# Order of the feed forward's units, and the layout of the weights' maxima on their way through DRAM

## The chip, the cores and the metric

The kernel runs on one core of one Trainium2 chip. The metric is the device time of one execution in microseconds (us); the median of three runs of the kernel before is 1657.21 us (1657.04 to 1657.3). Five engines work at once, each through its own instructions in order: TensorE (PE, matrix products; its weight loads are listed as PEld), VectorE (DVE), ScalarE (ACT), GpSimd (POOL) and SyncE (SP), which here issues every transfer. They meet through semaphores.

## The reference

One transformer block with conditioning, over 2048 rows of 512 values. Three steps are cut to what matters:

```
mod = silu(c) @ w_mod, cut into sa, ca, ga, sb, cb, gb
h = layernorm(x) * (1 + ca) + sa
q = h @ wq                                   # 32 heads of 128
p = softmax(q k^T / sqrt(128))               # over the last 512 rows of the cache, per head
x = x + ga * (concat(p v) @ wo)
h = layernorm(x) * (1 + cb) + sb
x = x + gb * ((gelu(h @ w_gate) * (h @ w_up)) @ w_down)      # 1376 hidden columns
```

## The kernel before, in words

**Precision.** Every operand of a product is held as two 16-bit halves, a high one and a low one, and a product is three matmuls: high by high, high by low, low by high. Before it is split, a weight matrix is scaled by a factor that depends on its largest absolute value. That maximum has to be known on all 128 partitions; bringing it there is called a crossing.

**Attention.** The 32 heads are taken in 16 groups of two, and the 2048 rows in four row groups of 512 (0 to 3). `slot` (L1294) runs the 128 pairs of a head and a row group as a pipeline: scores, row maxima (DVE), exponentials (ACT), the low half of the probabilities (POOL, tile `pp`), a transpose by transfer (SP, tile `pT`), the product with v two slots later, the product with wo three slots later, and the sum into `acc` (DVE). While one group of heads runs, the weights of the next are loaded into `raw`, their maxima are taken (`h_max` L649, into `mx`), crossed, and the weights scaled (`h_scale` L750) and split.

**The crossings.** From the third group of heads on, a crossing goes through DRAM. `h_send` (L663) writes four columns of maxima, one per matrix, of 128 partitions to a DRAM tile `most` of 128 rows of four values. `spread_max` (L667) reads the 512 values back to every partition (tile `sa`, 256 KB), reduces each kind's 128 values to one (tile `top`, four values on each partition), and makes the scale and its inverse from them (`iv` and `av`). There are two for each of 14 groups of heads (wq with k, v with wo) and one for the feed forward's weights (`ff_cross` L1255, `ff_scalars` L1269), 29 in all.

**Feed forward.** The 1376 hidden columns are 11 blocks f of 128 (the last of 96). Row groups 0 and 1 form pair 0, 2 and 3 pair 1. Blocks 0 and 1 of pair 0 are computed plainly (`fill`). All else is done in units (p, f): one block f for both row groups of a pair p, by seven products of halves in place of eight (Strassen's scheme in Winograd's form; `product` L1558, `stage` L1678). A unit is 7 x 6 = 42 matmuls. It needs the weights of its block as seven pieces with high and low halves, tile `aw`, of which three exist at a time (L1479, in the ring `pT`). `aw_load` brings gate and up weights in, and `aw_make` (L1822) scales two tiles, makes four sums on POOL, six high halves on ACT and six low halves on POOL. The left-hand pieces of a pair (tiles named B.. and T..) come from the second layer norm of its row groups; for pair 1 these steps are entered with units (0,2), (0,3) and (0,4) (`P1`, L1843).

The results of a unit become hidden tiles (`hid`, a ring of eight places, L1341). When both blocks of f and f + 1 of a pair are done, eight down steps (f, f + 1) by w_down are queued, one for each 128 rows, each of 6 matmuls and one sum into `acc` on DVE. After each of the four stages of a unit, one down step is taken from the queue (`down`, L1720). Blocks 0 to 3 of pair 1 are put through another scheme, in seven steps for two blocks.

The loop over `UNITS` (L1851) says for each unit which weights are made in it: `SPLIT` lists the units that have weights of their own, and a unit with index k in `SPLIT` makes those of index k + 2 and loads those of k + 4, unless `MAKE` says otherwise. A unit of pair 1 that isn't in `SPLIT` uses the weights of the same block of pair 0 (`AW[u if u in AW else (0, f)]`).

**What sets the order.** The program doesn't issue instructions as it goes. A planner (class `Weaver`) collects all of them with their dependencies and an estimated length each (`cost` L150), plays the whole program through on a model of the engines in several stages (`CUTS` L95) with a fixed number of turns and of random shakes from a fixed seed, and then issues the best order that it found (`issue` L412). Operations given with two engines (`either`, `tt`) get one of the two in that play. So the profile shows one line, L444, for nearly all instructions, and one reads it by the names of tiles. The rings of tiles and of PSUM banks tie the order of units: a unit's products use `psS`, of which two exist. Whatever changes in the program changes the input of the planner, and the order anywhere may change with it.

Of the kernel before, what the change touches and what calls it, by code (L numbers as in the profile page):

```python
# [10 lines left out]
F32 = mybir.dt.float32  # L11
# [3 lines left out]
OP = mybir.AluOpType  # L15
AX = mybir.AxisListType
PSUM = bass.MemoryType.PSUM

P = 128
# [10 lines left out]
NF = (DFF + P - 1) // P  # L30
# [15 lines left out]
ROUND = 1.0 + 2.0 ** -7  # L46
# [405 lines left out]
def adaln_block(ctx: ExitStack, tc: tile.TileContext, x, k_cache, v_cache, wq, wo,  # L452
                w_gate, w_up, w_down, c_in, w_mod, out):
    nc = Weaver(tc.nc, tc)
# [7 lines left out]
    dram = nc.pool(ctx.enter_context(tc.tile_pool(name="dram", bufs=1, space=bass.MemoryType.DRAM)), True, True)  # L462
# [7 lines left out]
    def small(pool, cols_, bufs=3, name="sm"):  # L470
        return pool.tile([P, cols_], F32, name=name, tag=name, bufs=bufs)
# [172 lines left out]
    HW, DG, IV, AV, ES, RV = {}, {}, {}, {}, {}, {}  # L644
# [16 lines left out]
            IV[kh], AV[kh] = iv[:, i:i + 1], av[:, i:i + 1]  # L661

    def h_send(which, m):  # L663
        t = DG[which[0]] = dram.tile([P, 4], F32, name="most", tag="most", bufs=3)
        nc.sync.dma_start(t, m[:, 0:4])

    def spread_max(t, top):  # L667
        w = right.tile([P, N], F32, name="sa", tag="sa", bufs=1)
        nc.sync.dma_start(w, t.rearrange("p a -> (p a)").partition_broadcast(P))
        r = small(base, 4, 2, "top")  # L670
        nc.vector.tensor_reduce(r, w.rearrange("p (k a) -> p a k", a=4), op=OP.max, axis=AX.X)
        iv, av = small(base, 8, 5, "iv"), small(base, 8, 5, "av")
        nc.vector.tensor_scalar(iv[:, 0:4], r, 1e-30, ROUND / top, op0=OP.max, op1=OP.mult)
        nc.vector.reciprocal(av[:, 0:4], iv[:, 0:4])
        return iv, av

    def h_spread(which):
        iv, av = spread_max(DG.pop(which[0]), WQS if which[0][0] in SETS[0] else WS)
        for i, kh in enumerate(which):
            IV[kh], AV[kh] = iv[:, i:i + 1], av[:, i:i + 1]  # L680
# [354 lines left out]
    def at(half, f, *a):  # L1035
        bg.setdefault(half, []).append((f, a))
# [43 lines left out]
    for g in range(1, NG):  # L1080
        b = 2 * PER * (g - 1)
        steps, cross_at = (STEPS, CROSS) if g > 1 else (EARLY, (EARLY_CROSS, (11, 13)))
        for i, kinds in enumerate(SETS):
            which = [(kind, g * G + n) for kind in kinds for n in range(G)]
            for m, (kind, h) in enumerate(which):
                st = steps[kind, h % G]
                at(b + st[0], load_raw, kind, h)
                if kind == "wo" and g >= GATED:
                    at(b + st[1], h_gate, h)
                at(b + st[1], h_max, (kind, h), mxs[i], m)  # L1090
                if (kind, h % G) == (kinds[-1], G - 1):
                    at(b + cross_at[i][0] + (g > 1) * 1.125, *((h_send, which, mxs[i]) if g > 1 else (h_cross_a, which, mxs[i])))
                    at(b + cross_at[i][1] + (g > 1) * 1.125, h_spread if g > 1 else h_cross_b, which)
                    for n in range(G):
                        at(b + cross_at[i][1] + (g > 1) * 1.25, h_scalars, g * G + n, ("qk", "vo")[i])
            for kind, h in which:
                st = steps[kind, h % G]
                at(b + st[2], h_scale, kind, h)
                if kind != "wq" or g < WINO:
                    at(b + st[3], h_split, kind, h)  # L1100
                if kind == "k":
                    at(b + st[4], h_turn, h)
        if g >= WINO:
            for half, f, nm in ((4, a_sum, "S1"), (5, a_split, "A1"), (5, a_sum, "S2"), (6, a_split, "S1"), (6, a_sum, "S3"),
                                (7, a_split, "S2"), (7, a_sum, "S4"), (8, a_split, "S3"), (8, a_split, "A22"),
                                (9, a_split, "S4")):
                at(b + half, f, g, nm)
# [147 lines left out]
    def ff_cross():  # L1255
        m = mxf
        for i in range(2):
            nc.vector.tensor_reduce(m[:, i:i + 1], mff[:, 12 * i:12 * i + 12], op=OP.max, axis=AX.X)
        nc.vector.tensor_reduce(m[:, 2:3], mff[:, 24:40], op=OP.max, axis=AX.X)
        for i in range(2):  # L1260
            nc.vector.tensor_reduce(m[:, 3 + i:4 + i], cols[:, 8 + 4 * i:12 + 4 * i], op=OP.max, axis=AX.X,
                                    apply_absolute_value=True)
        nc.vector.tensor_tensor(m[:, 3:4], m[:, 3:4], m[:, 4:5], op=OP.add)
        h_send(("f", "f", "f", "f"), m)
# [4 lines left out]
    def ff_scalars(part):  # L1269
        ab, t = ffs[:, 6:7], ffs[:, 7:8]  # L1270
        if part == 0:
            FS["iv"], av = spread_max(DG.pop("f"), WS)
            nc.vector.tensor_scalar_mul(ffs[:, 0:2], av[:, 0:2], 0.5)
            nc.vector.tensor_scalar_mul(ffs[:, 2:3], av[:, 2:3], 0.5)
            nc.vector.tensor_scalar(ab, FS["iv"][:, 3:4], WS, 1e-25, op0=OP.mult, op1=OP.max)
        iv = FS["iv"]
        if part == 1:
            nc.vector.tensor_scalar(ffs[:, 3:4], ab, iv[:, 0:1], 2.0 / HS, op0=OP.mult, op1=OP.mult)
            nc.vector.tensor_scalar(t, ab, iv[:, 0:1], 2.0, op0=OP.mult, op1=OP.mult)
            nc.vector.tensor_scalar(ffs[:, 5:6], ab, iv[:, 1:2], 4.0 * HID / HS, op0=OP.mult, op1=OP.mult)  # L1280
            nc.vector.tensor_scalar(ffs[:, 5:6], ffs[:, 5:6], iv[:, 2:3], t, op0=OP.mult, op1=OP.mult)
        if part == 2:
            nc.vector.tensor_scalar_mul(t, t, HID)
            nc.vector.reciprocal(ffs[:, 4:5], t)
            nc.vector.reciprocal(ffs[:, 8:9], ab)
            nc.vector.tensor_scalar(cols[:, 8:16], cols[:, 8:16], ffs[:, 8:9], HS, op0=OP.mult, op1=OP.mult)
# [53 lines left out]
    PLAIN = 2  # L1340
# [160 lines left out]
    def aw_load(u):  # L1501
        ff_load(u[1], u)
# [257 lines left out]
    for c, (a, b, d) in enumerate(((15.5, 15, 16.25), (15, 16.25, 16.5), (16.5, 16, 17.25), (16, 17.25, 17.5))):  # L1760
        at(e + a, ln2_chunk, 0, c)
        at(e + b, ln2_high, 0, c)
        at(e + d, ln2_low, 0, c, nc.gpsimd)
    UNITS = [(0, f) for f in range(PLAIN, 8)] + [(1, 6), (1, 7)] + [(p, f) for f in range(8, NF - 1) for p in range(2)] + \
        [(0, NF - 1)] + [(1, f) for f in range(6)] + [(1, NF - 1)]
    MAKE = {(0, 7): None, (1, 7): 7, (0, 8): 8, (0, 9): 9, (0, 10): 10}
    SPLIT = [u for u in UNITS if not (u[0] and 6 <= u[1] < NF - 1)]
    at(e + 10, aw_load, UNITS[0])
    at(e + 11, aw_load, UNITS[1])
    at(e + 16, aw_scale, UNITS[0])  # L1770
    for n in range(4):
        at(e + 17, aw_sum, UNITS[0], n)
    for n, nm in enumerate(AWS):
        h = (18.5, 18, 19.5, 19, 20.5, 20, 21.5, 21)
        at(e + h[n], aw_high, UNITS[0], nm)
        at(e + h[n + 1], aw_low, UNITS[0], nm)
# [45 lines left out]
    def aw_make(u):  # L1822
        aw_scale(u)
        for n in range(4):
            aw_sum(u, n)
        for nm in AWS:
            aw_high(u, nm)
            aw_low(u, nm)
# [22 lines left out]
    for n, u in enumerate(UNITS):  # L1851
        p, f = u
        k = SPLIT.index(u) if u in SPLIT else None
        k = MAKE.get(u, None if k is None else k + 2)
        if k is not None:
            if k + 2 < len(SPLIT):
                aw_load(SPLIT[k + 2])
            if k < len(SPLIT):
                aw_make(SPLIT[k])
        if WDS:  # L1860
            w = WDS.pop(0)
# [63 lines left out]
```

## Time and profile before

| | |
|---|---|
| median of three runs | 1657.21 us |
| the profiled execution, its own time | 1657.58 us |
| its span | 1655.8 us |
| mean granted TensorE clock | 0.997 |
| waits of TensorE from 1340 us on | 0.6 us on POOL (B), 0.5 us on ACT (r), 0.4 us on DVE (r) |
| waits of TensorE from 200 to 1300 us | 0.2 us on the transfer pT |
| sends of maxima (`most`) / spreads (`sa`) | 29 / 29 |
| median from issue to landing, send / spread | 1.9 us (28 of them) / 3.8 us |
| DVE's waits for a spread | 7.2 us, 8 times |

The span is the profiled execution from its first to its last instruction. "A <- B" in a wait says that A waited for B. In groups of instructions, "x29 | 31.6, 1089" is the count, the busy time in us and the mean length in ns, and what follows is idle time of the engine ahead of them and what ended it. Lines in order of time begin with the start and the length in us, and a bracket gives the idle time ahead. A matmul is listed with 379 ns because it overlaps with its neighbours; what one takes of TensorE's time is read from the count in a stretch without idle.

### The profile page before, as it was taken

What the parts mean: (1) busy time and instruction counts of PE and PEld (TensorE: products, weight loads), DVE (VectorE), ACT (ScalarE), POOL (GpSimd) and SP (SyncE); (2) the same over time, 40 slices, a digit from 0 to 9 for tenths busy, and PEclk for the clock granted to TensorE, in tenths of its full rate; (3) what the DMA queues carried; (4) which work ended last, traced back from release to release, by engine and by line L of the source; (5) the groups of instructions that cost most, each with busy time, mean ns of one, the idle gap of its engine ahead of it and who ended that gap; (6) DMA issues with size and microseconds to landing.
All of it is one profiled execution on the core that took longest, in us unless ns stands there. A gap on an engine that the chain in (4) does not pass through costs nothing.

```text
span 1655.8 us, 24293 instructions
## 1 busy us (share of the span) xinstructions
PE 1642.4 (99%) x7732; PEld 764.5 (46%) x7732; DVE 1289.3 (78%) x2381; ACT 1216.6 (73%) x2418; POOL 1305.0 (79%) x1097
## 2 busy tenths in 40 slices
PE   8999999999999999999999999999999999999999
PEld 4444444444444444444444444444444444444455
DVE  7777787878787788788999887888887956656557
ACT  5987797777787777888778777787878876545451
POOL 5999986868586878787768889999977898784682
PEclk9999999999999999999999999999999999999999
DMA  7676697878787778999999997788877712101111
GB/s 241 128 144 130 135 157 143 152 138 149 144 143 140 153 136 157 186 196 194 196 200 205 189 167 148 147 175 179 168 129 158 144 28 64 42 25 51 42 45 52
DMA packets 686289, 228.61 MB, mean 138 GB/s; under 512 B 596432, under 2 KB 663056, under 8 KB 686160
## 3 DMA queue, kind: packets, MB, share of 16 engines
q1 hardware_dynamic: 686160, 227.05, 69.1%
q8 instruction: 61, 1.00, 0.3%
q14 instruction: 68, 0.56, 0.1%
HBM read 78.98 MB, written 5.38 MB: 51 GB/s over the span
## 4 chain that ended last, share of the span: by engine, by line
PE 91%; ACT 2%; POOL 2%; DVE 2%; DMA 1%; SPq 1%; issue 1%; DVEq 0%; POOLq 0%; ACTq 0%
PE psS L444 31%; PE psW L444 23%; PE psO L444 21%; PE psQ L444 17%; SPq L444 1%; DVE st L444 1%; DVE acc L444 1%; DMA pT<-pp 1%; ACT p L444 0%; POOL pp L444 0%; POOL B L444 0%; DMA wm<-in_w_mod_dram 0%; POOL aw L444 0%; ACT T L444 0%; DMA raw<-in_B_w_up_dram 0%
## 5 line engine op out<-in xcount | busy, mean ns | idle before, releaser
L444 POOL TENSOR_TENSOR pp<-p,pp 128x1024 f16<-128x1024 f32 x256 | 545.9, 2132 | 212.8 <-ACT pp L444 97.3
L444 ACT ACTIVATE p<-psS,st,es 128x512 f32<-128x512 f32 x512 | 393.4, 774 | 187.7 <-DVE st L444 186.8
L444 DVE SCALAR_TENSOR_TENSOR acc<-psW,st,acc 128x512 f32<-128x512 f32 x496 | 367.2, 742 | 79.8 <-PE psW L444 77.7
L444 PE MATMUL psW<-wo,oT 128*128 128x512 f16 x1536 | 416.3, 379 | 0.0
L444 PE MATMUL psS<-kT,q 128*128 128x512 f16 x1536 | 379.1, 379 | 2.0 <-ACT q L444 2.0
L444 PE MATMUL psO<-pT,v 128*128 128x512 f16 x1536 | 377.1, 379 | 0.3 <-DMA pT<-pp 0.2
L444 DVE TENSOR_REDUCE st<-psS 128x2 f32<-128x1024 f32 x256 | 312.5, 1221 | 60.0 <-PE psS L444 59.6
L444 ACT ACTIVATE pp<-p 128x1024 f16<-128x1024 f32 x256 | 271.0, 1059 | 3.7
L444 PEld LDWEIGHTS <-q 128*128 128x128 f16 x1536 | 149.9, 98 | 182.1 <-ACT q L444 2.6
L444 PEld LDWEIGHTS <-v 128*128 128x128 f16 x1536 | 150.0, 98 | 181.3 <-DMA pT<-pp 1.2
L444 PEld LDWEIGHTS <-oT 128*128 128x128 f16 x1536 | 150.2, 98 | 180.1 <-DVE oT L444 0.5
L444 PEld LDWEIGHTS <-aw 128*128 128x128 f16 (+1 forms) x840 | 84.2, 100 | 95.1 <-issue 2.0
L444 ACT ACTIVATE oT<-psO 128x512 f16<-128x512 f32 x128 | 76.1, 594 | 66.2 <-PE psO L444 66.1
L444 PE MATMUL psQ<-T,S 128*128 128x512 f16 x504 | 123.3, 379 | 0.0
L444 PE MATMUL psQ<-B,A 128*128 128x512 f16 x480 | 119.6, 381 | 0.1
L444 PE MATMUL psS<-T,aw 128*128 128x512 f16 (+1 forms) x480 | 116.9, 379 | 0.0
L444 DVE SCALAR_TENSOR_TENSOR oT<-psO,oT 128x512 f16<-128x512 f32 x128 | 88.0, 688 | 30.9 <-ACT oT L444 30.6
L444 PEld LDWEIGHTS <-A 128*128 128x128 f16 x696 | 68.3, 98 | 83.3 <-issue 2.3
L444 PEld LDWEIGHTS <-S 128*128 128x128 f16 x672 | 65.8, 98 | 79.3
L444 ACT ACTIVATION_READ_ACCUMULATOR p<-psS,st,es 128x1 f32 x512 | 101.0, 197 | 0.0
L444 POOL TENSOR_TENSOR q<-h,q 128x512 f16<-128x512 f32 x84 | 97.5, 1161 | 2.0 <-ACT q L444 1.8
L444 DVE TENSOR_REDUCE mx<-raw 128x1 f32<-128x512 f32 x128 | 84.2, 674 | 15.6 <-DMA raw<-in_A_wq_dram 9.1
(211 smaller groups left out, 2295.6 us busy)
## 6 DMA issues: line engine op xcount, KB each, us to landing
raw<-in_A_k_cache_dram SPq DMA_DIRECT2D x32, 256.0 KB, 3.9
raw<-in_A_wq_dram SPq DMA_DIRECT2D x32, 256.0 KB, 3.7
raw<-in_A_v_cache_dram SPq DMA_DIRECT2D x32, 256.0 KB, 3.3
raw<-in_A_wo_dram SPq DMA_DIRECT2D x32, 256.0 KB, 3.2
pT<-pp SPq DMA_TRANSPOSE x512, 3.3
sa<-most SPq DMA_DIRECT2D x29, 256.0 KB, 3.8
raw<-in_B_w_gate_dram SPq DMA_DIRECT2D x24, 256.0 KB, 3.1
raw<-in_B_w_up_dram SPq DMA_DIRECT2D x24, 256.0 KB, 3.4
```

The costliest lines, as they stand in the source:

```text
L444: made[n] = real(*a, **k)
```

## The change: what it does

Two edits in one.

The units of the feed forward come in another order. Before: (0,2) to (0,7), (1,6), (1,7), (0,8), (1,8), (0,9), (1,9), (0,10), (1,0) to (1,5), (1,10). After: (0,2) to (0,9), (1,8), (1,9), (0,10), (1,6), (1,7), (1,0) to (1,5), (1,10). The units of pair 1 that use the weights of pair 0 are then (1,8) and (1,9), in place of (1,6) to (1,9); (1,6) and (1,7) are loaded and made once more. `SPLIT` has 18 entries in place of 16, and `MAKE` is written anew: no weights are made in (0,9) and in (1,8), those of (1,6) in (1,9), and from there on one set in each unit as long as there are any.

The DRAM tile of a crossing is laid out by kind: four rows of 128 values in place of 128 rows of four. The send writes each value by itself to its place, the read back is the same 512 values in a row, and the reduction takes 128 neighbours for each kind where it took every fourth value. The scale `iv` is computed by POOL, not by DVE; its inverse `av` stays on DVE.

```diff
     def h_send(which, m):
-        t = DG[which[0]] = dram.tile([P, 4], F32, name="most", tag="most", bufs=3)
-        nc.sync.dma_start(t, m[:, 0:4])
+        t = DG[which[0]] = dram.tile([4, P], F32, name="most", tag="most", bufs=3)
+        nc.sync.dma_start(t.rearrange("a p -> p a"), m[:, 0:4])
 
     def spread_max(t, top):
         w = right.tile([P, N], F32, name="sa", tag="sa", bufs=1)
-        nc.sync.dma_start(w, t.rearrange("p a -> (p a)").partition_broadcast(P))
+        nc.sync.dma_start(w, t.rearrange("a p -> (a p)").partition_broadcast(P))
         r = small(base, 4, 2, "top")
-        nc.vector.tensor_reduce(r, w.rearrange("p (k a) -> p a k", a=4), op=OP.max, axis=AX.X)
+        nc.vector.tensor_reduce(r, w.rearrange("p (a k) -> p a k", a=4), op=OP.max, axis=AX.X)
         iv, av = small(base, 8, 5, "iv"), small(base, 8, 5, "av")
-        nc.vector.tensor_scalar(iv[:, 0:4], r, 1e-30, ROUND / top, op0=OP.max, op1=OP.mult)
+        nc.gpsimd.tensor_scalar(iv[:, 0:4], r, 1e-30, ROUND / top, op0=OP.max, op1=OP.mult)
         nc.vector.reciprocal(av[:, 0:4], iv[:, 0:4])
...
-    UNITS = [(0, f) for f in range(PLAIN, 8)] + [(1, 6), (1, 7)] + [(p, f) for f in range(8, NF - 1) for p in range(2)] + \
-        [(0, NF - 1)] + [(1, f) for f in range(6)] + [(1, NF - 1)]
-    MAKE = {(0, 7): None, (1, 7): 7, (0, 8): 8, (0, 9): 9, (0, 10): 10}
-    SPLIT = [u for u in UNITS if not (u[0] and 6 <= u[1] < NF - 1)]
+    UNITS = [(0, f) for f in range(PLAIN, NF - 1)] + [(1, NF - 3), (1, NF - 2), (0, NF - 1), (1, 6), (1, 7)] + \
+        [(1, f) for f in range(6)] + [(1, NF - 1)]
+    MAKE = {(0, 9): None, (1, 9): 9}
+    SPLIT = [u for u in UNITS if not (u[0] and NF - 3 <= u[1] < NF - 1)]
```

## The prediction

> **What bounds the kernel now.** I read the page's totals first, then the busy time in stretches of 40 us, then TensorE's own waits in the feed forward, then the groups of instructions there, and last the transfers of the crossings.
>
> ```profile
> span 1655.8 us, 24293 instructions
> PE 1642.4 (99%) x7732; PEld 764.5 (46%) x7732; DVE 1289.3 (78%) x2381; ACT 1216.6 (73%) x2418; POOL 1305.0 (79%) x1097
> ...
> PE 91%; ACT 2%; POOL 2%; DVE 2%; DMA 1%; SPq 1%; issue 1%; DVEq 0%; POOLq 0%; ACTq 0%
> ```
>
> TensorE works for 1642.4 of 1655.8 us, and 91% of the chain that ended last is its own work. It idles 13.4 us in all. Where, the stretches tell (columns: stretch, its length, then the busy time and count of each engine, granted clock, DMA share, GB/s):
>
> ```profile
> 0.00:40.00 40.00, 33.54 (x156) 20.08 (x156) 29.06 (x76) 20.76 (x35) 20.25 (x40) 0.91 0.80 250
> 40.00:80.00 40.00, 38.88 (x195) 19.66 (x196) 32.77 (x66) 39.87 (x80) 37.53 (x31) 1.00 0.69 128
> ...
> 600.00:640.00 40.00, 40.00 (x187) 18.11 (x185) 31.79 (x60) 29.73 (x62) 31.49 (x25) 1.00 0.75 144
> ...
> 1320.00:1360.00 40.00, 39.40 (x199) 19.77 (x197) 27.16 (x47) 31.15 (x54) 36.29 (x40) 1.00 0.22 54
> ...
> 1440.00:1480.00 40.00, 39.03 (x180) 17.39 (x178) 25.40 (x33) 21.03 (x40) 32.13 (x31) 1.00 0.10 27
> ...
> 1640.00:1680.00 40.00, 11.84 (x55) 5.17 (x53) 8.94 (x14) 0.63 (x1) 0.00 (x0) 0.95 0.14 53
> ```
>
> The start loses 6.46 + 1.12 = 7.58 us, before any instruction that the change touches. The last matmul ends at 1651.84, and 1655.8 - 1651.84 = 3.96 us of last sums and stores follow. The stretch from 600 stands for the attention: no idle, 187 matmuls in 40 us, so 0.214 us each. The feed forward loses 0.60 us near 1345 and 0.97 us after 1440, 1.57 us together. What is left, 13.4 - 7.58 - 3.96 - 1.57 = 0.3 us, is spread over 1240 us of attention. The change neither adds nor takes a matmul, so **its whole reach is the waits: about 1.6 us at best, 0.1% of the time**, unless it makes new ones.
>
> TensorE's longest wait from 1340 on, then the two waits after 1440 in order of time with the POOL work beside them:
>
> ```profile
> PE psS L444 <- POOL B L444: 0.6, 1, 0.6
> ```
>
> ```profile
> 1353.88 0.59 PE L444 MATMUL psS<-B,aw 128*128 128x512 f16 x2
> ...
> 1462.95 1.46 PE L444 MATMUL psS<-B,aw 128*128 128x512 f16 x6 [0.39 <-DVE r L444]
> ...
> 1463.61 1.16 POOL L444 TENSOR_TENSOR T<-ft,T 128x512 f16<-128x512 f32 x1
> ...
> 1467.51 0.81 PE L444 MATMUL psS<-B,aw 128*128 128x512 f16 x3 [0.52 <-ACT r L444]
> ```
>
> The waits of 0.39 and 0.52 us stand in units (1,6) and (1,7), the first two of the second pair. POOL is still writing that pair's T tiles at 1464.77, while their products run; the down steps that could fill the gap had been spent. The wait of 0.60 us is on a tile of the plain blocks, ahead of the first unit, which starts at 1353.88.
>
> **The order of units.** The change puts (0,8) and (0,9) ahead of the second pair's first unit, which becomes (1,8). A unit is 42 matmuls, 42 x 0.214 = 9.0 us, and four down steps of 6 matmuls, 5.1 us. So the T tiles are due 2 x 14.1 = 28 us later, and both waits lose their cause: **-0.91 us**; with the 0.05 us beside them -0.97, which I take. Not below zero gain by this edit, not above 1.57.
>
> Pair 1's units (1,6) and (1,7) no longer share weights with (0,6) and (0,7), so two sets more are loaded, scaled, summed and split. Rows of the feed forward's groups:
>
> ```profile
> L444 POOL TENSOR_TENSOR aw<-raw,aw 128x512 f16<-128x512 f32 x14 | 17.2, 1232 | 23.3 <-ACT aw L444 14.9 <-DVE r L444 7.5 <-ACT r L444 0.9
> L444 ACT ACTIVATE raw<-raw,ffs 128x512 f32<-128x512 f32 x23 | 16.1, 709 | 0.4 <-DMA raw<-in_B_w_up_dram 0.4
> L444 POOL TENSOR_TENSOR S1f<-raw 128x256 f32<-128x256 f32 x13 | 11.2, 860 | 3.3 <-issue 1.3 <-ACT r L444 1.2 <-POOL aw L444 0.7
> L444 POOL TENSOR_TENSOR aw<-S4f,aw 128x256 f16<-128x256 f32 x14 | 10.3, 737 | 2.4 <-DVE r L444 1.8 <-DVE hf L444 0.6
> L444 ACT ACTIVATE aw<-raw 128x512 f16<-128x512 f32 x14 | 8.7, 623 | 11.1 <-PE psS L444 11.0
> L444 ACT ACTIVATE aw<-S3f 128x256 f16<-128x256 f32 x14 | 5.7, 409 | 1.1 <-POOL S3f L444 0.9
> ```
>
> POOL, each set: four sums at no more than 0.860, one low half at 1.232, five at no more than 0.737: 8.4 us. ACT: two scalings at 0.709, one high half at 0.623, five at 0.409: 4.1 us. Two sets: 16.8 us of POOL, 8.2 of ACT. They fall in (1,9) and (0,10), since the ring of three weight tiles frees a place only when (1,8) and then (1,9) are through: nine units of 14.1 us after 1353.9, from about 1481 on. What stood there before, and what the busiest stretch stood:
>
> ```profile
> 1354.00:1431.00 77.00, 77.00 (x372) 36.70 (x370) 47.72 (x67) 51.10 (x95) 65.15 (x77) 1.00 0.17 47
> 1431.00:1470.00 39.00, 38.03 (x175) 16.99 (x174) 24.59 (x33) 18.89 (x34) 32.60 (x30) 1.00 0.10 28
> 1470.00:1500.00 30.00, 30.00 (x141) 13.60 (x139) 17.30 (x24) 15.88 (x31) 20.76 (x28) 1.00 0.19 51
> 1500.00:1530.00 30.00, 30.00 (x141) 14.04 (x139) 19.82 (x27) 17.81 (x35) 12.58 (x17) 1.00 0.16 44
> 1530.00:1570.00 40.00, 40.00 (x187) 18.74 (x186) 20.50 (x29) 18.44 (x37) 25.35 (x33) 1.00 0.13 37
> ```
>
> POOL (the fifth count and the time ahead of it) is free for 17.4 + 14.7 = 32 us from 1500 to 1570 and a part of the 9.2 us ahead of them; 16.8 us fit. From 1354 to 1431, POOL at 65.15 of 77 us (85%) with a set made in nearly every unit cost TensorE nothing. So I take **0**; without that cover it is what the 84% of 1431:1470 cost, 0.97 us. The four loads join DMA engines that are at most 0.19 busy there; the four issues on SP stand two units ahead of their use. 0.
>
> The down queue no longer stands empty in one unit, as it did in (0,9), so four steps fewer are left behind the last unit. The last product and the first matmul on the last unit's hidden tile:
>
> ```profile
> 1631.89 1.46 PE L444 MATMUL psS<-T,aw 128*96 128x512 f16 x6
> ...
> 1640.89 0.68 DVE L444 TENSOR_TENSOR hid<-r,hid 96x512 f16<-96x512 f32 x1
> ...
> 1645.85 0.81 PE L444 MATMUL psO<-wd,hid 96*128 96x512 f16 x3
> ```
>
> The cover is 1645.85 - 1633.35 = 12.5 us; less 4 x 6 x 0.214 = 5.1 it is 7.4. The first hidden tile was ready at 1641.57, 8.2 us after the product, with additions of the down steps in between on DVE; four of those go too. I take **0**; by the order as it stands it would cost 0.8 us.
>
> **The crossings.** All 29 are off TensorE's path unless a queue holds. Sending the maxima becomes 512 single values in place of 128 runs of four; the reduction reads neighbours; one line of four values moves from DVE to POOL.
>
> ```profile
> L444 DVE TENSOR_REDUCE mx<-raw 128x1 f32<-128x512 f32 x128 | 84.2, 674 | 15.6 <-DMA raw<-in_A_wq_dram 9.1 <-DMA raw<-in_A_k_cache_dram 4.8 <-POOL raw L444 1.1
> L444 DVE TENSOR_REDUCE top<-sa 128x4 f32<-128x512 f32 x29 | 31.6, 1089 | 7.3 <-DMA sa<-most 7.2
> L444 DVE TENSOR_SCALAR iv<-top 128x4 f32<-128x4 f32 x29 | 6.1, 211 | 0.0
> ...
> L444 POOL TENSOR_SCALAR nmr<-nmr 128x4 f32<-128x4 f32 x8 | 1.6, 205 | 0.4
> ```
>
> ```profile
> msum<-gb SPq DMA_DIRECT2D x2, 256.0 KB, 4.2
> most<-mx SPq DMA_DIRECT2D x28, 2.0 KB, 1.9
> ...
> msu<-mall SPq DMA_DIRECT2D x2, 2.0 KB, 3.1
> ```
>
> The reduction falls from 1.089 towards 0.674 us, the length of a reduction over 512 neighbours: DVE gains 29 x (0.415 + 0.211) = 18 us, POOL takes 29 x 0.205 = 6 us. Neither engine bounds: 0. The send's landing has no row. From below it is the 1.9 us of now; from above the 4.2 us of a scatter of 256 KB; I take 3.1, the read of 512 single values, its nearest kin. The spread's load waits on SP for that landing, and behind it wait the transposes for the P V products. The closest of the 29 pairs of issues:
>
> ```profile
> 321.66 0.53 SPq L444 DMA_DIRECT2D most<-mx  x1
> 324.99 0.53 SPq L444 DMA_DIRECT2D sa<-most  x1
> ```
>
> 324.99 - 321.66 = 3.33 us, so a landing at 3.1 holds SP nowhere: **0**. At 4.2 it holds it 7 times, at most 0.87 us and 3.4 us in all. What such a hold does, the longest wait of DVE for a crossing shows:
>
> ```profile
> 996.40 1.10 DVE L444 TENSOR_REDUCE top<-sa 128x4 f32<-128x512 f32 x1 [2.16 <-DMA sa<-most]
> ...
> 998.95 2.13 POOL L444 TENSOR_TENSOR pp<-p,pp 128x1024 f16<-128x1024 f32 x1 [2.15 <-issue]
> ```
>
> DVE stood 2.16 us, POOL then 2.15, and no wait of TensorE follows: a cover of at least 2.2 us. The moved line adds two hand-overs: POOL waits for the reduction, and DVE's reciprocal waits for POOL, at worst behind one pp subtraction, 2.13 + 0.21 = 2.3 us; queued behind the reciprocal are the row maxima. Just past the cover at the worst place, so 0 again.
>
> [...]
>
> **Sum.** The profiled execution took 1657.58 us (span 1655.8 and 1.78 around it). 1657.58 - 0.97 = 1656.6; it lies 0.37 above the median of the runs, 1657.21, so the forecast is **1656.2 us**. The order of all engines is computed anew from the changed program, so small waits may move anywhere; this is in the range.
>
> **Rivals.** B, the gain comes back: the sets made back to back from 1481 cost the 0.97 us again, and the shorter end its 0.8: 1657.2 + 0.8 = 1658.0. For it, POOL's load; against it, 1354 to 1431. C, the send holds SP: were the landing to grow with the packets, 4 x 1.9 = 7.6 us, 25 of the 29 pairs would hold SP, 69.6 us together and 19.9 of them past a cover of 2.16: 1657.2 + 19.9 = 1677, slower. It decides from a landing of 3.33 + 2.16 = 5.5 us. Against it, 3.1 and 4.2 us. D, POOL's new wait: at the 8 crossings where DVE already waits 7.2 us in sum, 2.34 more each, less 2.16 of cover each, is 7.2 + 8 x 0.18 = 8.7: 1665.9, slower.
>
> ```profile
> DVE top L444 <- DMA sa<-most: 7.2, 8, 2.2
> ```
>
> E, the new order also loses the 0.60 us at 1345 and the 1.12 after 40: 1656.2 - 1.72 = 1654.5.
>
> **Chances.** Forecast 0.56, B 0.22, E 0.10, C 0.07, D 0.05. The range from 1654.4 to 1660.0 holds the forecast, B and E, with 2 us above B for waits of the new order; about 0.15 lies outside. A measurement tells 0.2%, 3.3 us, from no change. Faster by that would be under 1653.9, beyond E: 0.04. Slower, over 1660.5, is C, D and a badly packed order: 0.13. The same: 0.83.
>
> **What would show it.** Right: no wait of TensorE for DVE or ACT r in the first two units of pair 1; 7732 matmuls; the reduction near 0.67 us; the send landing near 3 us and no SP wait on it over 1 us. Wrong: waits of TensorE on pT or q in the attention (C, D), on aw or hid from 1481 on (B), or a start that differs by over 1 us.

## The result, and the profile after

The changed kernel takes 1791.97 us (median of four runs, 1787.8 to 1793.63) where the kernel before took 1657.12 us (four runs, 1656.26 to 1657.3): a ratio of 1.0811, with a 95% interval of 1.0795 to 1.0827. The forecast was 1656.2 us with a range up to 1660.0. The profiled execution took 1792.95 us, its span is 1791.1.

The totals of the profile after: the span, the busy time, share and count of each engine, and the queue that carries the kernel's transfers, with its packets, MB and the time of its packets as a share of 16 DMA engines.

```profile
span 1791.1 us, 24223 instructions
...
PE 1684.3 (94%) x7732; PEld 773.2 (43%) x7732; DVE 1274.7 (71%) x2349; ACT 1235.0 (69%) x2446; POOL 1318.1 (74%) x1137
...
q1 hardware_dynamic: 699408, 228.10, 75.4%
```

The same queue in the profile before:

```profile
q1 hardware_dynamic: 686160, 227.05, 69.1%
```

TensorE still does 7732 matmuls. It idles 1791.1 - 1684.3 = 106.8 us where it idled 13.4, which is 93.4 more. It is also busy 1684.3 - 1642.4 = 41.9 us longer with the same matmuls. Most of that is a lower clock: by the trace's clock records TensorE was busy for 79.4 us at a granted clock of 0.50 where it was for 6.3, and half of the difference is 36.6 us. The rest, some 5 us, is about what the ends of matmuls would make that no neighbour overlaps any more (an estimate: 0.379 - 0.214 = 0.165 us at each of 35 more gaps, 5.8 us). Idle and busy together make the 135.3 us by which the span grew. The DMA engines have 75.4% of 1791.1 = 1350 us of packet time where they had 69.1% of 1655.8 = 1144. That is 206 us more for 1 MB more.

Where it happens, the stretches tell. First before, then after (columns: stretch, its length, busy time and count of PE, PEld, DVE, ACT and POOL, granted clock, DMA share, GB/s):

```profile
0.00:200.00 200.00, 192.42 (x908) 93.98 (x909) 149.21 (x309) 155.36 (x301) 175.46 (x159) 0.98 0.72 155
200.00:1340.00 1140.00, 1139.73 (x5295) 518.20 (x5294) 946.48 (x1804) 896.77 (x1809) 911.84 (x695) 1.00 0.84 162
```

```profile
0.00:200.00 200.00, 192.68 (x908) 94.81 (x909) 150.47 (x309) 156.22 (x303) 177.00 (x162) 0.98 0.76 154
200.00:1340.00 1140.00, 1050.75 (x4682) 465.20 (x4681) 826.23 (x1565) 796.61 (x1608) 808.22 (x628) 0.96 0.93 146
```

Up to 200 us both kernels have done 908 matmuls. From 200 to 1340, in the attention with its crossings, the kernel after does 4682 instead of 5295. The missing 613, at the 0.214 us of an undisturbed matmul, are 131 us. So nearly the whole loss lies in the attention, which the edit touches only in the crossings (the planner may have moved other work there too; the experiments below hold the order fixed). The feed forward, from the first unit's first product to the end of the span, takes 1655.8 - 1353.88 = 301.9 us before and 1791.1 - 1490.34 = 300.8 us after.

The transfers of the crossings after (KB each, median us from issue to landing), with the nearest kin that the prediction used:

```profile
sa<-most SPq DMA_DIRECT2D x29, 256.0 KB, 4.6
...
msu<-mall SPq DMA_DIRECT2D x2, 2.0 KB, 2.7
...
most<-mx SPq DMA_DIRECT2D x28, 2.0 KB, 9.4
```

**The send of the maxima lands after 9.4 us, where it landed after 1.9.** (The trace has the landing of 20 of the 28 sends; the median is theirs.) Who waits for it, in the waits of SP's queue, of all engines, and of TensorE alone (us in total, times, longest):

```profile
SPq L444 <- DMA most<-mx: 109.5, 24, 6.5
```

```profile
DVE top L444 <- DMA sa<-most: 126.6, 23, 8.2
...
POOL iv L444 <- DVE top L444: 103.1, 19, 8.6
```

```profile
PE psW L444 <- DVE acc L444: 44.3, 15, 5.4
PE psQ L444 <- DVE h L444: 20.7, 7, 3.4
PE psO L444 <- DMA pT<-pp: 19.9, 12, 5.9
PE psQ L444 <- DVE q L444: 6.2, 2, 4.1
```

SP waited 0.4 us for a send in all before, and 109.5 us now; DVE waited 7.2 us for the spreads, and 126.6 now. The four waits of TensorE make 91.1 of its 106.8 us of idle. Three of them are on DVE and one on the transposes, the two things that stand behind a crossing in an in-order queue.

One crossing of each kind. A hold on SP and the DMA engines, in SP's issues in order of time and TensorE's next product:

```profile
214.00 0.37 SPq L444 DMA_DIRECT2D most<-mx  x1
214.47 2.62 SPq L444 DMA_TRANSPOSE pT<-pp  x2
...
218.39 8.72 SPq L444 DMA_TRANSPOSE pT<-pp  x2
227.22 0.53 SPq L444 DMA_DIRECT2D sa<-most  x1
```

```profile
225.79 1.44 PE L444 MATMUL psO<-pT,v 128*128 128x512 f16 x3 [5.94 <-DMA pT<-pp]
```

The spread was issued 13.2 us after the send; before, the closest of the 29 pairs were 3.33 us apart. Half of it is no wait for the landing: the issue of the first of the two transposes at 218.39 alone took 6.67 us, with a median of 1.33 for the five from 214 to 228. Transposes that were issued right behind the send came late, and TensorE stood 5.94 us for one. The same time in stretches of 2 us:

```profile
216.00:218.00 2.00, 2.00 (x11) 0.92 (x10) 1.48 (x4) 2.00 (x6) 1.83 (x1) 1.00 2.29 177
218.00:220.00 2.00, 1.85 (x9) 0.65 (x7) 2.00 (x5) 1.97 (x4) 0.50 (x2) 1.00 1.13 3
220.00:222.00 2.00, 0.00 (x0) 0.00 (x0) 0.16 (x2) 1.71 (x5) 2.00 (x2) 1.00 1.84 10
222.00:224.00 2.00, 0.00 (x0) 0.00 (x0) 0.00 (x0) 0.00 (x0) 1.03 (x1) 1.00 1.64 24
224.00:226.00 2.00, 0.21 (x1) 0.14 (x2) 0.00 (x0) 0.00 (x0) 0.00 (x0) 0.51 0.80 162
226.00:228.00 2.00, 2.00 (x6) 0.71 (x5) 0.00 (x0) 0.00 (x0) 0.00 (x0) 0.50 1.17 299
...
230.00:232.00 2.00, 2.00 (x9) 0.84 (x8) 0.85 (x2) 1.12 (x2) 0.93 (x1) 0.78 1.21 238
```

Two things are to be seen. From 218 to 224 the DMA engines are listed as more than fully busy (shares of 1.13 to 1.84: a packet counts with its whole time in the stretch in which it starts) and move 3 to 24 GB/s, against 177 just before. The long packets are not the send's own. By the trace's packet records a burst of 4-byte packets goes out from 214.91 to 215.27 us, 7 to 9 ns each; from 218 to 223.5 us it is packets of 256 bytes, the size of the transposes' packets, that last 555 ns at the median, where the median of the run is 18 ns. So the small writes are gone early, and what follows them stands. And around the gap's end the granted clock falls to 0.50, from 224.05 to 230.88 us: 6 matmuls in 2 us where the undisturbed stretch at 216 has 11. The half clock begins 4.2 us into the gap of 5.94 us and lasts 6.83 us. Shorter gaps have it too: the clock records of this run have 18 such stretches in the attention, 11 of 3.41 us and 7 of 6.83, one for each of the 16 gaps of TensorE of 2.76 us and more, begun from 2.0 us before the gap's end to 1.3 after it, as with the one of 2.95 us below (half clock from 299.15 to 302.56 us), and two behind gaps of 2.06 and 2.26 us, while seven others of 2.14 to 2.73 us were not followed by any. What makes the difference between these is not shown. So many of the long holds are paid twice, as idle time and as slow matmuls behind it.

The hold of DVE, at a crossing sent at 284.02:

```profile
298.46 0.69 DVE L444 TENSOR_REDUCE top<-sa 128x4 f32<-128x512 f32 x1 [6.57 <-DMA sa<-most]
```

```profile
299.80 1.44 PE L444 MATMUL psQ<-B,A 128*128 128x512 f16 x3 [2.95 <-DVE h L444]
```

DVE stood 6.57 us before the reduction. The combination `h`, queued on DVE behind the reduction, was what TensorE then lacked for 2.95 us.

### The profile page after: what moved, and what is told of

It is laid out like the page before. It is cut to its first block, busy times and chain, and to the rows that moved or that the text cites. A ratio compares the mean times of both kernels' runs of the same rounds, so it can differ in the third digit from the quotient of the medians.

```text
span 1791.1 us, 24223 instructions
## 1 busy us (share of the span) xinstructions
PE 1684.3 (94%) x7732; PEld 773.2 (43%) x7732; DVE 1274.7 (71%) x2349; ACT 1235.0 (69%) x2446; POOL 1318.1 (74%) x1137
## 2 busy tenths in 40 slices
DMA packets 699536, 229.65 MB, mean 128 GB/s; under 512 B 607632, under 2 KB 676304, under 8 KB 699408
## 3 DMA queue, kind: packets, MB, share of 16 engines
q1 hardware_dynamic: 699408, 228.10, 75.4%
## 5 line engine op out<-in xcount | busy, mean ns | idle before, releaser
L444 POOL TENSOR_TENSOR pp<-p,pp 128x1024 f16<-128x1024 f32 x256 | 545.1, 2129 | 209.3 <-ACT pp L444 134.5
L444 ACT ACTIVATE p<-psS,st,es 128x512 f32<-128x512 f32 x512 | 393.1, 773 | 250.0 <-DVE st L444 247.0
L444 PE MATMUL psW<-wo,oT 128*128 128x512 f16 x1536 | 461.0, 386 | 44.5 <-DVE acc L444 44.3
L444 DVE SCALAR_TENSOR_TENSOR acc<-psW,st,acc 128x512 f32<-128x512 f32 x496 | 367.6, 742 | 94.8 <-PE psW L444 93.0
L444 PE MATMUL psO<-pT,v 128*128 128x512 f16 x1536 | 405.2, 387 | 22.1 <-DMA pT<-pp 19.9
L444 PE MATMUL psS<-kT,q 128*128 128x512 f16 x1536 | 403.7, 384 | 0.3 <-DMA kT<-k 0.2
L444 DVE TENSOR_REDUCE st<-psS 128x2 f32<-128x1024 f32 x256 | 312.2, 1219 | 63.0 <-PE psS L444 62.0
L444 ACT ACTIVATE pp<-p 128x1024 f16<-128x1024 f32 x256 | 270.9, 1058 | 3.9
L444 PEld LDWEIGHTS <-oT 128*128 128x128 f16 x1536 | 151.8, 99 | 230.6 <-issue 56.0
L444 PEld LDWEIGHTS <-v 128*128 128x128 f16 x1536 | 152.0, 100 | 214.1 <-issue 29.1
L444 PEld LDWEIGHTS <-q 128*128 128x128 f16 x1536 | 151.8, 99 | 192.5 <-issue 17.4
L444 PE MATMUL psQ<-B,A 128*128 128x512 f16 x480 | 131.2, 392 | 21.4 <-DVE h L444 20.7
L444 PE MATMUL psQ<-T,S 128*128 128x512 f16 x504 | 132.3, 387 | 6.7 <-DVE q L444 6.2
L444 PEld LDWEIGHTS <-aw 128*128 128x128 f16 (+1 forms) x840 | 84.3, 100 | 93.8 <-issue 0.4
L444 PE MATMUL psS<-T,aw 128*128 128x512 f16 (+1 forms) x480 | 117.0, 379 | 0.3 <-ACT h L444 0.3
L444 ACT ACTIVATE oT<-psO 128x512 f16<-128x512 f32 x128 | 75.7, 591 | 53.1 <-PE psO L444 52.5
L444 PEld LDWEIGHTS <-A 128*128 128x128 f16 x696 | 69.2, 99 | 99.7 <-issue 21.8
L444 DVE TENSOR_REDUCE top<-sa 128x4 f32<-128x512 f32 x29 | 19.9, 685 | 126.7 <-DMA sa<-most 126.6
L444 DVE SCALAR_TENSOR_TENSOR oT<-psO,oT 128x512 f16<-128x512 f32 x128 | 87.9, 687 | 29.6 <-ACT oT L444 28.3
L444 PEld LDWEIGHTS <-S 128*128 128x128 f16 x672 | 67.1, 100 | 95.5 <-issue 20.0
L444 POOL TENSOR_SCALAR iv<-top 128x4 f32<-128x4 f32 x29 | 6.6, 228 | 130.4 <-DVE top L444 103.1
L444 ACT ACTIVATION_READ_ACCUMULATOR p<-psS,st,es 128x1 f32 x512 | 101.1, 197 | 0.0
```

The costliest lines, as they stand in the source:

```text
L444: made[n] = real(*a, **k)
```

## The experiments

Two questions: which of the three parts of the change costs the time, and why the send takes 9.4 us. For the second, the prediction's rival C had the landing grow with the number of packets; whether it is that, or where the values are written, was open. In the diffs `+` is what an experiment adds to the kernel that it starts from.

**The layout alone**, on the kernel before. Every instruction of every engine stands in the same order as before. Only the form of the send and the elements that the reduction takes together differ, so nothing else is changed.

```diff
-        t = DG[which[0]] = dram.tile([P, 4], F32, name="most", tag="most", bufs=3)
-        nc.sync.dma_start(t, m[:, 0:4])
+        t = DG[which[0]] = dram.tile([4, P], F32, name="most", tag="most", bufs=3)
+        nc.sync.dma_start(t.rearrange("a p -> p a"), m[:, 0:4])
...
-        nc.vector.tensor_reduce(r, w.rearrange("p (k a) -> p a k", a=4), op=OP.max, axis=AX.X)
+        nc.vector.tensor_reduce(r, w.rearrange("p (a k) -> p a k", a=4), op=OP.max, axis=AX.X)
```

> The layout by kind alone (512 single values sent, reduction over neighbours), the scale on DVE, units as before. Theory 1: 1775 to 1800 us, the send landing after 9 us or so. Theory 2 (POOL's wait in the crossing, 103 us in the changed kernel, is the cause): under 1680 us, since POOL no longer waits for the reduction itself.

Measured: 1781.84 us against 1657.47, a ratio of 1.0748 (1.0728 to 1.0768). The send's landing and DVE's and TensorE's waits in its profile:

```profile
most<-mx SPq DMA_DIRECT2D x28, 2.0 KB, 9.2
```

```profile
DVE top L444 <- DMA sa<-most: 118.0, 23, 8.0
...
PE psO L444 <- DMA pT<-pp: 44.9, 16, 7.0
...
PE psW L444 <- DVE acc L444: 32.1, 19, 4.6
```

The layout alone costs 124 us, by the same waits.

**The whole change without the layout.** Here all instructions stand in the order of the kernel after; only the send's form and the reduction that goes with it are those of before.

```diff
-        t = DG[which[0]] = dram.tile([4, P], F32, name="most", tag="most", bufs=3)
-        nc.sync.dma_start(t.rearrange("a p -> p a"), m[:, 0:4])
+        t = DG[which[0]] = dram.tile([P, 4], F32, name="most", tag="most", bufs=3)
+        nc.sync.dma_start(t, m[:, 0:4])
...
```

> The whole change but the layout: new order of units, scale on POOL, 128 runs of four sent as before. Theory 1: 1655 to 1658 us, and so all but the layout is worth under 0.1%. Theory 2: over 1690 us.

Measured: 1657.63 us against 1657.47, a ratio of 0.9999 (0.999 to 1.0008). With the send as it was, the new order of units and the line on POOL cost nothing, in the very order of instructions that takes 1791.97 us with the new send. Its queue:

```profile
q1 hardware_dynamic: 688272, 228.10, 68.9%
```

The kernel after has 699408 packets, 11136 more, which is 29 x 384: 512 packets for each send where there were 128.

The two results settle where the loss is: in the layout. It costs 124 us in the order of before and 134 us in that of after. Whether the 10 us between them come from POOL, which also waits there, or from the other order can't be told from these runs.

**The units alone**, on the kernel before.

```diff
-    UNITS = [(0, f) for f in range(PLAIN, 8)] + [(1, 6), (1, 7)] + [(p, f) for f in range(8, NF - 1) for p in range(2)] + \
+    UNITS = [(0, f) for f in range(PLAIN, NF - 1)] + [(1, NF - 3), (1, NF - 2), (0, NF - 1), (1, 6), (1, 7)] + \
...
```

> The new order of the units alone, crossings as before. Theory 1 (the loss is all in the send of single values): about 1656.2 us, the waits of 0.39 and 0.52 us in the first units of pair 1 gone. Rival (the new order of the units costs by itself): over 1660 us.

Measured: 1659.73 us against 1657.47, a ratio of 1.0013 (1.0005 to 1.0022). TensorE's waits from 1345 us on:

```profile
PE psS L444 <- POOL B L444: 0.9, 1, 0.9
```

The waits of 0.39 and 0.52 us in the first units of pair 1 are gone, and what is left in the feed forward is the wait for `B`, 0.9 us where it was 0.6; yet the time is 2.3 us longer, and not the 1656.2 us that was expected.

**The line on POOL alone**, on the kernel before.

```diff
-        nc.vector.tensor_scalar(iv[:, 0:4], r, 1e-30, ROUND / top, op0=OP.max, op1=OP.mult)
+        nc.gpsimd.tensor_scalar(iv[:, 0:4], r, 1e-30, ROUND / top, op0=OP.max, op1=OP.mult)
```

> The scale on POOL alone, layout and units as before. Theory 1: 1655 to 1659 us, POOL waiting for the reduction under 15 us in sum. Theory 2: over 1690 us.

Measured: 1663.94 us against 1657.47, a ratio of 1.0041 (1.0025 to 1.0056), above the 1655 to 1659 expected; POOL waits 24.0 us for the reduction, also more than expected. The same line together with the units cost nothing, though POOL waits 32.5 us for the reduction there, so the question became whether such tenths of a per cent belong to the edits or to the order that the planner happens to find. The next three runs start it from another seed: with nothing else changed, with the line on POOL, and with the units.

```diff
-        draw = random.Random(7)
+        draw = random.Random(8)
```

> The kernel before with another seed in the planner's random shakes, nothing else: what another order of the same work is worth. If the 0.4% of the scale on POOL is an accident of order, this moves by as much, 3 to 8 us either way; if orders are alike, it stays within 1655 to 1659 us.

> The other seed and the scale on POOL, units and layout as before. If POOL's wait in the crossing costs by itself: 5 to 8 us over the other seed alone. If order alone made the 0.4%: within 4 us of the other seed alone, either side.

> The other seed and the new order of units, crossings as before. My theory of the units (about 1 us gained in the first units of pair 1, the rest accident of order): within 4 us of the other seed alone, and no wait of TensorE over 1 us after the first unit begins.

Measured, each against 1657.35 us: the other seed alone 1659.56 (1.0011, 1.0001 to 1.002), with the line on POOL 1657.69 (1.0002, 0.9992 to 1.0012), with the units 1657.15 (0.9998, 0.9988 to 1.0007). So the seed alone moves the time by 2 us, less than the 3 to 8 that were set as the sign of an accident of order, and from the other seed neither edit costs anything. With the other seed POOL waits 29.5 us for the reduction, more than the 24.0 of the run that lost 0.41%, so the length of that wait doesn't set the loss. In that run TensorE's waits after the start are small ones on DVE (`oT`, `q`, `h`, `acc`), 0.2 us of them for a crossing's own result (`av`). That the order made the 0.41% fits this and is not shown further.

**The sends in runs of two.** The kernel after, with 256 runs of two values in place of 512 single ones and the reduction to match; all instructions stand in the same order.

```diff
-        t = DG[which[0]] = dram.tile([4, P], F32, name="most", tag="most", bufs=3)
-        nc.sync.dma_start(t.rearrange("a p -> p a"), m[:, 0:4])
+        t = DG[which[0]] = dram.tile([2, P, 2], F32, name="most", tag="most", bufs=3)
+        nc.sync.dma_start(t.rearrange("b p a -> p b a"), m[:, 0:4].rearrange("p (b a) -> p b a", b=2))
...
```

> The changed kernel with the send cut into 256 runs of two values in place of 512 single ones (two kinds side by side in DRAM, the reduction adapted). Theory A (each separate write has its price): the landing falls from 9.4 to about 1.9 + (9.4 - 1.9) x 128 / 384 = 4.4 us, the time to between 1655 and 1680 us. Theory B (a fixed price as soon as a partition's four values don't stay one run): landing near 9 us, time over 1750 us.

Measured: 1659.29 us against 1657.09, a ratio of 1.0015 (1.0004 to 1.0026).

```profile
most<-mx SPq DMA_DIRECT2D x28, 2.0 KB, 3.4
```

At a landing of 3.4 us, close to the 3.1 that the prediction assumed, the time stays within the forecast's range, and SP waits for a send once, 0.9 us.

**The plan told of the price.** The kernel after, with a DMA time of 7 us for the send in the planner, where its formula gives at most 10 ns (4 x 4 x 128 / 195); the kernel's own work is the same.

```diff
-            n = 1450.0 if what != "dma_start" else n * 4 * P / (195.0 if short else 390.0)
+            single = what == "dma_start" and a[0].name.startswith("most")
+            n = 1450.0 if what != "dma_start" else 7000.0 if single else n * 4 * P / (195.0 if short else 390.0)
```

> The changed kernel, 512 single values sent, but the planner is told that this transfer keeps the DMA engines for 7 us. Theory C (the loss is that queues wait in order for a landing that the plan has too early): the time falls below 1680 us, DVE's wait for the spread below 30 us. Theory D (the single writes keep the DMA engines busy, and the transposes behind them come late whatever the plan): the time stays over 1720 us, with TensorE waiting for pT.

Measured: 1664.01 us against 1657.09, a ratio of 1.0046 (1.0027 to 1.0066). Its transfers, its queue, and the waits for them (a line was added to the kernel, so L444 is L445 here):

```profile
most<-mx SPq DMA_DIRECT2D x28, 2.0 KB, 10.4
```

```profile
q1 hardware_dynamic: 699408, 228.10, 81.0%
```

```profile
PE psO L445 <- DMA pT<-pp: 4.3, 4, 1.7
DVE top L445 <- DMA sa<-most: 3.5, 3, 2.3
```

The sends are as long as in the kernel after, 10.4 us, and the packets take as much of the DMA engines, 81.0% of 1662.5 = 1347 us. But the spreads now follow their sends by 11.9 us and more, so nothing stands in a queue for them: DVE waits 3.5 us in place of 126.6. **The loss is not the time of the send by itself. It is that an order in which a spread could follow its send after 3.33 us ran with a landing of 9 us**, on engines that take their work in order.

**What makes the send long.** Probes beside the crossings of the kernel before, each a write of the same 512 values by other paths, with their own landing in the DMA table. The plan is told that a probe is long, which spreads the program; the time of the whole (1724.0 and 1670.5 us, one run each) is no result.

```diff
+        shape = {"pA": [4, P], "pB": [4, P, 16], "pC": [2, P, 2], "pD": [P, 4, 2]}[kind]
+        t = dram.tile(shape, F32, name=kind, tag=kind, bufs=2)
...
+            dst, PT_[i] = t.rearrange("a p -> p a"), t[0:1, :].rearrange("a p -> p a")
...
+            dst, PT_[i] = t[:, :, 0].rearrange("a p -> p a"), t[0:1, :, 0].rearrange("a p -> p a")
...
+        nc.sync.dma_start(dst, src)
```

> The kernel before, with its own send of 128 runs of four, and after each crossing one more write of the same 512 values that nothing in the crossing waits for, in one of four forms by turns: pA, single values laid out by kind as in the change; pB, single values 64 bytes apart; pC, 256 runs of two by kind; pD, single values 8 bytes apart, a partition's four side by side. A single value read back and times 0 added keeps them in place. Theory A (price for each separate write): pA, pB and pD land alike, after 8 to 10 us, pC after 4 to 5. Theory E (price for neighbours that different partitions write, as in pA): pB lands under 4 us, pA near 9.

```profile
most<-mx SPq DMA_DIRECT2D x28, 2.0 KB, 2.0
pA<-mx SPq DMA_DIRECT2D x7, 2.0 KB, 8.8
pB<-mx SPq DMA_DIRECT2D x7, 2.0 KB, 2.8
pC<-mx SPq DMA_DIRECT2D x6, 2.0 KB, 4.2
pD<-mx SPq DMA_DIRECT2D x6, 2.0 KB, 4.0
```

pA is the change's own send, by kind, each value next to those of the neighbouring partitions: 8.8 us. pB writes the same 512 single values, in the same order, with 64 bytes from each to the next: 2.8 us. So a price for each separate write alone, which was the reason given with rival C, falls: 512 writes can land in 2.8 us. The packet records of pA and pB begin alike: in both the small packets, 9 ns each, leave mostly within 1 to 2 us of the issue. The difference arises after they have left. pC is runs of two, pD is single values 8 bytes apart. The second set fills the row in:

```diff
+        shape = {"pA": [4, P], "pF": [4, P, 4], "pG": [4, P, 8], "pH": [P, 4]}[kind]
...
+        elif kind in ("pF", "pG"):
+            dst, PT_[i] = t[:, :, 0].rearrange("a p -> p a"), t[0:1, :, 0].rearrange("a p -> p a")
+        else:
+            dst, src, PT_[i] = t, m[:, 0:8].rearrange("p (a b) -> p a b", b=2)[:, :, 0], t[:, 0:1]
```

> Probes again, four other forms by turns: pA as before; pF, single values 16 bytes apart by kind; pG, single values 32 bytes apart by kind; pH, single values packed as the kernel before packs its runs, a partition's four side by side with no gap. Theory F (about 0.5 us for each separate write into the same 64 bytes: 16 in pA, 4 in pF, 2 in pG, 16 in pH): pA near 9, pF near 2.8, pG near 2.8, pH near 9 us. Theory G (only neighbours from different partitions hold each other up): pH under 5 us, pF between 3 and 9 us.

```profile
pA<-mx SPq DMA_DIRECT2D x7, 2.0 KB, 9.6
pF<-mx SPq DMA_DIRECT2D x7, 2.0 KB, 4.0
pH<-mx SPq DMA_DIRECT2D x6, 2.0 KB, 7.9
pG<-mx SPq DMA_DIRECT2D x6, 2.0 KB, 3.0
```

pF has its values 16 bytes apart, pG 32. pH packs 512 single values densely, but with the four of a partition side by side, as the send of before has them in one run. It still takes 7.9 us, so it isn't that neighbours come from different partitions. (In this run the trace lacks some landings: pA and pF have four of seven, pG five of six, and pH only two of six, 6.9 and 8.9 us.) By the distance from one single write to the next: 4 bytes 7.9 to 9.6 us, 8 bytes 4.0, 16 bytes 4.0, 32 bytes 3.0, 64 bytes 2.8. At 512 writes the landing follows **how densely the separate writes lie in DRAM**. Their number counts as well: 128 runs of 16 bytes side by side land in 2.0 us, 512 single values 16 bytes apart in 4.0, with equally many writes to a stretch. It isn't proportional (8 and 16 bytes are alike), pF missed the 2.8 us expected from a fixed price for each write into the same 64 bytes, and with 512 writes in each form, distance and total length can't be told apart. What in the memory or on the way to it makes dense writes slow stays open.

## Why the prediction was wrong

**The step that failed** is the term of the send: "The send's landing has no row … I take 3.1, the read of 512 single values, its nearest kin", with 1.9 and 4.2 us as its ends. It measured 9.4 us, and the hold that the sum put at 0 for it came to 109.5 us of SP's waiting and, by the two experiments on the layout, 124 to 134 us of time. The kin was a read. The read of 512 single values lands in 2.7 us in the kernel after as well; it is the writing of neighbouring values that costs, and no row of the kernel before showed such a write. Both ends were taken from transfers of another kind, and an end taken so doesn't bound. With a landing of 3.4 us (runs of two) the kernel took 1659.29 us, inside the forecast's range though 3.1 us above the forecast.

**Rival C was the mechanism, with too small a price.** "The send holds SP" is what the trace shows, past the point of 5.5 us that it gave. Its 7.6 us of landing was near, by luck: its reason, growth with the packets, was wrong, as pB showed. Its price of 19.9 us was too small by a factor of nearly seven, in three ways:

- It laid the hold on SP alone and took 2.16 us of cover off each crossing, since DVE once stood that long without a wait of TensorE. That row gave a lower bound of the cover at one place, and was used as the cover everywhere. In the kernel after DVE stands 126.6 us for 23 spreads, 5.5 us each, with `acc`, `h` and `q` queued behind.
- It left out that a send of 9 us also delays transfers behind it that don't wait for its value. Behind the send at 214.00 five transposes were issued up to 228 us; the trace has the landing of three, 9.9, 9.8 and 3.9 us after the issue, and the median of such transposes before was 3.3 us. The packet records above show packets of the transposes' size standing in that time, 555 ns each at the median where the median of the run is 18; why they stood behind the small writes is not shown. The row of these transposes:

```profile
DMA to landing us min/median/max: 3.9/9.8/9.9
```

- It had no term for the clock: some 37 of the 135.3 us are the same matmuls at a granted clock of 0.50 behind the gaps.

**Rival D, POOL's new wait**, isn't what cost the time: with the old send POOL's line costs nothing in two orders (1657.63 us with the units, 1657.69 with the other seed). In the third, from the first seed, 1663.94 us came near D's 1665.9, but with a shorter wait of POOL than in the order with the other seed. In the kernel after POOL waits 103.1 us for the reduction, but as a consequence of the late spread.

**What was right.** The reduction over neighbours, in the groups of the kernel after (busy us, mean ns, then idle us before them):

```profile
L444 DVE TENSOR_REDUCE top<-sa 128x4 f32<-128x512 f32 x29 | 19.9, 685 | 126.7 <-DMA sa<-most 126.6
```

The reduction takes 685 ns (forecast 674) in place of 1089, the line on POOL 228 ns (forecast 205), and no run shows a gain of time from it, as said. In the feed forward the waits in the first two units of pair 1 are gone. The two additional sets of weights cost TensorE no wait on `aw`, and the cover at the end shrank to 1780.68 - 1773.51 = 7.2 us (forecast 7.4) without one. TensorE's waits from 1440 us on (the first two stand ahead of the first unit, the third, at 1766, in the last), and the rows of that cover, the last product and the first matmul on the last unit's hidden tile:

```profile
PE psS L444 <- POOL B L444: 0.6, 1, 0.6
PE psS L444 <- DVE r L444: 0.5, 1, 0.5
PE psS L444 <- ACT h L444: 0.3, 1, 0.3
```

```profile
1490.34 0.81 PE L444 MATMUL psS<-B,aw 128*128 128x512 f16 x3
```

```profile
1773.13 0.38 PE L444 MATMUL psS<-T,aw 128*96 128x512 f16 x1
...
1780.68 0.38 PE L444 MATMUL psO<-wd,hid 96*128 96x512 f16 x1
```

The gain of 0.97 us can't be told from the runs: a new order moves the time by 2 us either way. From the first matmul of a unit, at 1490.34, to the end, the feed forward is 1.1 us shorter, which is of the size forecast and no more than one profiled execution of each.

**The chances.** Rival C had 0.07. Two rows pointed the other way, and both were of transfers that don't write single values next to each other. An operation that no row shows, in a chain that everything waits for in order, deserved ends as far apart as the ignorance was: at 7.6 us, which the prediction had worked out itself, the range would have held a slower kernel, though not yet this one.

## What to carry to other kernels

When a transfer changes from runs to single values, ask first whether it writes or reads, and whether the values lie next to each other in DRAM: reading 512 of them one by one landed in 2.7 us in the kernel after, writing them 64 bytes apart or in runs of 16 bytes in 1.9 to 2.8 us, writing them densely one by one in 7.9 to 10.4. In a schedule that is packed for given latencies, on engines that work in order, a transfer off TensorE's path that lands 7 us later can cost TensorE itself: here 134 us for 29 sends, 4.6 us each. Here it held its queue (109.5 us of SP's waits), the queue of the engine that waits for it (126.6 us of DVE's), the transfers behind it (transposes landed after 9.9 and 9.8 us where the median was 3.3) and, behind long gaps of TensorE (two of nine from 2.06 to 2.73 us and all 16 longer ones in the attention of this run), the clock (some 37 us). If a plan sets the order, its price for a changed operation is part of the change: told of it, the same sends cost 0.46% in place of 8.1%.

## What the runs showed of the hardware that was not expected

- Dense single writes of 4 bytes to DRAM: 512 of them land in 7.9 to 10.4 us (medians of six sets of sends), 64 bytes apart in 2.8 us, 256 runs of 8 bytes in 3.4 to 4.2 us, 128 runs of 16 bytes in 1.9 to 2.2 us. The first adds to the DMA engines' listed time: over the same kernel with the old send (68.9% of a span of 1657.9 us) the 29 sends add 1350 - 1142 = 208 us of all 16 engines' packet time, 7.2 us each. By the packet records 186 us of it stand in packets of 256 bytes, not in the writes of 4 bytes, whose median stays 9 ns. Runs of two (69.8% of 1660.1 us) add 17 us, 0.6 each.
- Before it lands almost nothing else moves: from 6 to 8 us after the issue of a send the DMA engines move 13 GB/s (median of the 29), against 166 in the same place with the old send in the same order of instructions.
- With a gap of 5.94 us on TensorE came 6.83 us at half clock; gaps of 2.06 and 2.26 us were followed by 3.41 us of it, seven of 2.14 to 2.73 us by none. Over the kernel the slower matmuls made some 37 us, more than a quarter of the loss.
